# Threshold attention and a gated feed-forward layer on one core: the start of the feed-forward work moved from slot 20 to slot 22

## The chip, the cores and the metric

The kernel runs on one NeuronCore of a Trainium2 chip. Five engines work beside each other, each through its own list of instructions: TensorE (PE; its weight loads are shown as PEld), VectorE (DVE), ScalarE (ACT), GpSimd (POOL), and SyncE (SP), which here only issues DMA transfers. They meet through semaphores. Matmul results land in PSUM, eight banks of 2 KB per partition; PE alone writes matmul results there, and DVE and ACT read them out. The metric is device time in microseconds (us) of one execution.

## The reference

For each of 8 batches and 8 heads, with 576 tokens and head size 64, in f32:

```
scores = q k^T / sqrt(64)
thresh = max(scores, last axis) - tau
scores = where(scores >= thresh, scores, -1e9)
attn   = softmax(scores)
x      = attn v                 -> tokens x 512   (4608 tokens in all)
h      = x @ w_in               (512 -> 2048)
out    = (h * clip(h + 3, 0, 6) / 6) @ w_out      (2048 -> 512)
```

## The kernel before

**Slots.** Heads are taken two at a time (a pair) and pairs two at a time (a quad); a batch has two quads, and there are 16 quads. Each quad is cut into 9 slots: slots 0 to 3 are the first four 128-row blocks of queries of its first pair, 4 to 7 those of its second pair, and slot 8 holds the last 64 rows of both pairs. So there are 144 slots, numbered `n` = 0 to 143, and one loop over them writes the instructions of every engine in an order fixed by hand (`manual_schedule`). Within an engine that order is kept exactly; there is no scheduler behind it.

**One slot of attention.** `scores` (L288) makes the 128x576 scores of both heads of a pair in PSUM. `sm_max` (L303, DVE) copies them to the SBUF tile `s` and takes the row maximum; there are two such scans per slot. `sm_bias` (L308, POOL) makes the threshold, `sm_mask` (L312, ACT) rejects what is below it, `sm_exp` (L317, ACT) takes the exponential and its sum, `sm_recip` (L320, DVE) inverts the sum, and `sm_norm` (L325, POOL) writes the normalised rows as bf16 into `pn`. The pools of `s` and `pn` have four buffers each. The rows must then be transposed to `pT` (or `pR` for a slot 8): either by a DMA transpose on SP's queue (L333), or, where `on_chip` holds (L479), by nine PE transposes into PSUM (`pe_transpose`, L340) two slots later and one DVE copy (L341) in the slot after that. `av` (L349, L352) multiplies `pT` with `v`; DVE evicts the result into `xT` (L360) or `xR` (L370).

**The feed-forward work.** `mm1` (L384; L379 for the odd 64-row tails) multiplies a block of `xT` with `w_in` into one PSUM bank. One such item is eight matmuls of 128x256. `mm1_relu` reads the bank on ACT in even slots (L392) and on DVE in odd slots (L394), and `mm1_gate` (L407, DVE) writes `g`. `mm2_part` (L418) is a quarter of a 128-token output tile: four matmuls of 128x512; `second` issues one or more such parts in an even slot. The items wait in the list `todo1`, the parts in `todo2`: eight items of a batch enter `todo1` when the last pair of the batch has been multiplied with `v`, the rest after its tails (`multiply`). What is left after slot 143 is done in a tail.

**The two stages.** `N1` divides the loop. Up to slot `N1` the scores of slot n+2 are made in slot n and there is no feed-forward work. From slot `N1` each slot takes one item from `todo1`, the products with `v` are issued inside the slot instead of at its end, and an odd slot makes the scores of the two slots ahead; from `N1`+3 the scores of odd slots go to other columns of PSUM (`first`, `score_col`), which touch the lower halves of banks 2 and 5. `N2` is the last even slot in which ACT takes the exponentials before the relu of that slot. Banks 2 and 5 serve in turn (`bank`) for products with `v` and for the transposes of q and k. An item's bank is `HB` (6), `OB` (7), or bank 2 or 5, as L582 and L583 say; the parts of `mm2` collect in `OB`.

**Data movement.** `loads` holds the loads of q and k, issued one group per slot on SP behind that slot's transpose; for the fifth quad a group is four transfers of small rows. `casts` and `vcasts` hold the casting loads of the weights and of v, issued on POOL's queue behind that slot's `sm_norm`.

**Around slot 20.** In this version the items run in slots 20 to 35, there is none left for slots 36 and 37, and from slot 38 on there is one in every slot. Parts of `mm2` run in even slots from slot 28: two each in 28, 30, 32 and 34, three in 36, one in 38, two in 40, one in 42 and one in 44, sixteen in all; from slot 46 two each. `quad 1`'s second pair is multiplied with `v` in two halves of 256 columns (slots 18 and 21) and its tails in slot 23.

Of the kernel before, what the change touches and what calls it, by code (L numbers as in the profile page):

```python
# [20 lines left out]
def kernel(  # L21
# [18 lines left out]
    NSLOT = 9  # L40
    NB = 2
    N0 = 3
    N1 = 20
    N2 = 26
    HB, OB = 6, 7
    scale = 1.0 / math.sqrt(D)
    tau = float(tau)
# [30 lines left out]
    casts = []  # L78
# [93 lines left out]
    def start(jobs, n):  # L172
        for _ in range(min(n, len(jobs))):
            jobs.pop(0)()
# [35 lines left out]
    now = -1  # L210
    turn = 0
# [5 lines left out]


    def copy_out(out, in_):
        if 0 <= now < N1 + 4:  # L220
            nc.vector.tensor_copy(out=out, in_=in_)
        else:
            nc.scalar.copy(out=out, in_=in_)
# [48 lines left out]
    def first(n):  # L272
        return n > N1 + 2 and n % 2 == 1

# [32 lines left out]
    def sm_bias(sl):  # L307
        nc.gpsimd.tensor_scalar(out=sl.bias[:], in0=sl.m[:], scalar1=-scale, scalar2=tau, op0=Alu.mult, op1=Alu.add)  # L308
# [6 lines left out]
    def sm_exp(sl, i):  # L315
        s = sl.s[:, i, :]
        nc.scalar.activation(out=s, in_=s, func=Act.Exp, accum_out=sl.rsum[:, i:i + 1])  # L317
# [57 lines left out]
    def mm1(item, hb=HB):  # L375
        b, ni, c0 = item
        if c0 is None:
            for ki in range(KI):
                nc.tensor.matmul(ps[:, hb, :], xR[b // 2][:, ki, :], w_in_sb[:, ki, ni * P:ni * P + 512],  # L379
                                 start=(ki == 0), stop=(ki == KI - 1))  # L380
        else:
            for n in range(2):
                for ki in range(KI):
                    nc.tensor.matmul(ps[:, hb, n * 256:(n + 1) * 256], w_in_sb[:, ki, (ni + n) * P:(ni + n + 1) * P],  # L384
                                     xT[b][:, ki, c0:c0 + 256], start=(ki == 0), stop=(ki == KI - 1))
        return ps[:, hb, :]
# [27 lines left out]
    def mm2_part(bb, mt, part, ob=OB):  # L414
        if part == 0:
            o_ps[0] = ps[:, ob, :]
        for ni in range(part * 4, part * 4 + 4):
            nc.tensor.matmul(o_ps[0], gbuf[:, ni, mt * P:(mt + 1) * P], w_out_sb[:, ni, :],  # L418
                             start=(ni == 0), stop=(ni == NI - 1))
# [14 lines left out]
    todo2 = []  # L434
# [39 lines left out]
    queue = []  # L474
    for quad in range(NQUAD):
        for slot in range(NSLOT):
            sl = Slot()
            sl.quad, sl.slot, sl.n = quad, slot, len(queue)
            sl.on_chip = len(queue) < N1 - 3 and (slot in (1, 3, 5, 7, 8) or slot == 0 and quad > 0)  # L479
            queue.append(sl)  # L480
    scores(0)
    sm_max(queue[0])
# [17 lines left out]
    for quad in range(NQUAD):  # L500
        p0, p1 = 2 * quad, 2 * quad + 1
        if quad < NB:
            jobs = (((8, p0, 0, 512), (9, p1, 0, 256), (12, p1, 256, 256), (14, None, 0, 0)) if quad else
                    ((8, p0, 0, 512), (13, p1, 0, 512), (15, None, 0, 0)))
        else:
            jobs = [(7 - quad % 2 + 2 * i, *of) for i, of in enumerate(
                ((p0, 0, 256), (p0, 256, 256), (p1, 0, 256), (p1, 256, 256), (None, 0, 0)))]
        for after, *of in jobs:
            products.setdefault(quad * NSLOT + after, []).append((quad, *of))
# [10 lines left out]

    def second():
        nonlocal pieces, bb, mt, part
        pieces = min(len(todo2), {36: 3, 38: 1, 42: 1, 44: 1}.get(now, 2)) if now % 2 == 0 else 0
        for _ in range(pieces):
            bb, mt, part = todo2.pop(0)
            mm2_part(bb, mt, part)
# [3 lines left out]
    pieces = bb = mt = part = 0  # L530
    waiting = []
    for n, sl in enumerate(queue):
        quad, slot = sl.quad, sl.slot
        b, g = divmod(quad, 2)
        now = n
        if slot in (0, 4):
            pts[2 * quad + slot // 4] = pt_pool.tile([P, 9, 512], BF16, tag="pT", name="pT")
        if slot == 8:
            ptr[quad] = ptr_pool.tile([P, 9, P], BF16, tag="pR", name="pR")
        for ahead in {0: (1, 2), 9: (3,), 16: (4,)}.get(n, (quad + 2,) if quad > 2 and slot == (2 if quad == 3 else 0) else ()):  # L540
            if ahead < NQUAD:
                load_quad(ahead)
        if slot == 0 and g == 1 and b + 1 < B:
            load_v(b + 1)
        for copy in last_keys:
            copy()
        last_keys = []
        if 0 < n <= N1:
            for i in range(2):
                sm_exp(prev, i)  # L550
        if n + 1 < len(queue):
            if n <= N1 or n > N2 + 1 or n % 2 == 0:
                sm_max(queue[n + 1])
            sm_bias(queue[n + 1])
        even = n >= N1 and n % 2 == 0
        if n >= N0:
            sm_recip(prev)
        for copy in waiting:
            copy()
        waiting = []  # L560
        if N0 <= n <= N1:
            scores(n + 2)
            if n in (3, 6):
                warm_up(6)
        if even and n <= N2:
            sm_max(queue[n + 2])
        if n == N1:
            for i in range(2):
                sm_mask(sl, i)
        exp_first = even and n <= N2  # L570
        if exp_first:
            for i in range(2):
                sm_exp(sl, i)
        if n == N1:
            for i in range(2):
                sm_mask(queue[n + 1], i)

        if todo1 and n >= N1:
            item, then = todo1.pop(0)
            if n == len(queue) - 2:  # L580
                second()
            h = mm1(item, 0 if n == len(queue) - 1 else HB if n <= N1 or n % 2 == 0 or pieces > 1 else  # L582
                    (2, 5)[turn % 2] if pieces else OB)  # L583
            todo2.extend(then)
        else:
            item = None
        if n >= N1:
            for copy in multiply(n):
                copy()
        if item:  # L590
            mm1_gate(item, h, mm1_relu(h, on_act=even))
        if n > 1 and queue[n - 2].on_chip:
            waiting.append(pe_transpose(queue[n - 2]))
        if prev is not None and n < N0:
            sm_recip(prev)
            for copy in waiting:
                copy()
            waiting = []
        if n != len(queue) - 2:
            second()  # L600
        if n < N1:
            for i in range(2):
                sm_mask(sl, i)
        if n >= N1:
            if not exp_first:
                for i in range(2):
                    sm_exp(sl, i)
            if n != N1 and n + 1 < len(queue):
                for i in range(2):
                    sm_mask(queue[n + 1], i)  # L610
        if n < N1:
            waiting.extend(multiply(n))
        if part == 3:
            waiting.append(lambda tile=(bb, mt): late.extend(mm2_out(*tile, on_act=False)))
            part = 0
        evict = []
        for job, of in turns.get(n, ()):
            if job == "k":
                (last_keys if even else evict).append(transpose_k(of))
            elif job == "q":  # L620
                if of // 2 not in qkT:
                    alloc_qk(of // 2)
                (waiting if even else evict).append(transpose_q(of))
            else:
                (last_keys if even else evict).append(transpose_rest(of, of_k=of > 0))
        evict = [out_of_psum for out_of_psum in evict if out_of_psum]
        if N0 <= n < N1:
            waiting.extend(evict)
            evict = []
        for out_of_psum in evict:  # L630
            out_of_psum()
        if n == 0:
            warm_up(8)
        if n < N0:
            scores(n + 2)
            warm_up(6)
        elif n > N1 and n % 2:
            for m in (n + 3, n + 2):
                if m < len(queue):
                    scores(m)  # L640
        if n > 0:
            sm_norm(prev)
        flush()
        if n == 0:
            start(loads, 5)
        elif n not in (4, 12, 15, 18, 21) and not 23 < n < 30 and (n < 37 or n % 2 == 0):
            start(loads, 1)
        if n < 4 or 15 < n < 20 or n > 33:
            start(vcasts, 1 if n < N1 or n % 2 else 0)
        else:  # L650
            start(casts, 2 if n in (5, 8, 11, 14) or N1 <= n < N1 + 7 else 1)
        prev = sl

    last = NQUAD - 1
# [85 lines left out]
```

## Time and profile before

| what | value |
|---|---|
| time, median of 3 runs (lowest, highest) | 519.51 us (519.31, 520.68) |
| the profiled execution: its time, its span | 519.51 us, 517.7 us |
| PE busy, mean granted clock | 505.2 us (98%), 0.999 |
| ACT busy | 450.8 us (87%) |
| DVE busy | 441.5 us (85%) |
| POOL busy | 298.1 us (58%) |
| DMA transposes on SP's queue (`pT`, `pR`) | 119 + 15 |

Busy time is time in which an instruction of that engine was under way. Matmuls overlap in the array and their ends are modelled, so PE at 98% is not PE at its peak; how long a stretch of work takes is read from the starts of the groups. DVE and ACT instructions also overlap by about 0.1 us: two exponentials of one slot start 0.67 us apart.

### The profile page before, as it was taken

The page shows a single profiled execution, that of the slowest core. Times are in us where ns is not written, and L with a number is a line of the kernel's source. Part 1 is how long each engine was busy: PE and PEld are TensorE (multiplying, and loading weights), DVE is VectorE, ACT ScalarE, POOL GpSimd, SP SyncE. Part 2 cuts the span into 40 slices and gives each one's busy share as a digit, 9 for nine tenths or more (in the row PEclk, how much of TensorE's full clock was granted, in tenths as well). Part 3 has the DMA queues.
Part 4 walks back from the last instruction along what each step waited for, and adds up shares of the span by engine and source line. Part 5 has one row for each costly group of instructions (what it writes and reads, how often), then busy time and mean ns, then how long its engine had stood idle before and what let it go on. Part 6 is the DMA issues. An engine that isn't in the chain of part 4 may idle for free.

```text
span 517.7 us, 12082 instructions
## 1 busy us (share of the span) xinstructions
PE 505.2 (98%) x4126; PEld 320.6 (62%) x4126; DVE 441.5 (85%) x1125; ACT 450.8 (87%) x977; POOL 298.1 (58%) x536
## 2 busy tenths in 40 slices
PE   8999998999999999999999999999999999999996
PEld 6655565666655666666655666666655666667564
DVE  3788988998999999999999999999999999877261
ACT  3999987999999999999999999999999999986060
POOL 1788877756665666657566656657566655552000
PEclk9999999999999999999999999999999999999999
DMA  6999999989999999999899998999989996654122
GB/s 139 175 160 156 157 164 181 180 145 179 154 171 183 167 194 162 171 163 177 157 159 175 177 175 157 174 155 175 171 152 168 187 179 115 104 121 89 63 56 68
DMA packets 317870, 79.65 MB, mean 154 GB/s; under 512 B 300432, under 2 KB 312976, under 8 KB 317808
## 3 DMA queue, kind: packets, MB, share of 16 engines
q1 hardware_dynamic: 298304, 68.85, 79.3%
q0 software_dynamic: 18304, 9.64, 15.0%
q8 instruction: 32, 0.52, 0.4%
q10 hardware_dynamic: 1200, 0.39, 0.3%
q14 instruction: 30, 0.25, 0.1%
HBM read 36.70 MB, written 9.44 MB: 89 GB/s over the span
## 4 chain that ended last, share of the span: by engine, by line
PE 79%; DVE 5%; DMA 2%; ACT 2%; POOL 0%; issue 0%; POOLq 0%; DVEq 0%
PE ps L288 25%; PE ps L418 23%; PE ps L384 19%; PE ps L349 7%; PE ps L379 2%; DVE g L407 1%; PE ps L352 1%; DMA pT<-pn 1%; DVE s L303 1%; DMA g<-go 1%; DVE r L394 1%; PE ps L663 1%; ACT r L392 1%; ACT s L312 1%; ACT s L317 0%
## 5 line engine op out<-in xcount | busy, mean ns | idle before, releaser
L325 POOL TENSOR_SCALAR pn<-s,rinv 128x576 bf16<-128x576 f32 x288 | 210.7, 743 | 21.5 <-issue 4.5
L303 DVE TENSOR_SCALAR_CACHE_REDUCE s<-ps 128x576 f32<-128x576 f32 x288 | 205.1, 749 | 19.6 <-PE ps L288 8.4
L312 ACT ACTIVATE s<-s,bias 128x576 f32<-128x576 f32 x288 | 205.8, 762 | 7.0 <-POOL bias L308 6.5
L317 ACT ACTIVATE s<-s 128x576 f32<-128x576 f32 x288 | 192.5, 671 | 0.3
L288 PE MATMUL ps<-kT,qT 64*128 64x192 f32 (+7 forms) x1280 | 177.4, 419 | 3.4 <-DVE s L303 1.9
L288 PEld LDWEIGHTS ps<-kT,qT 64*128 64x128 f32 (+1 forms) x1280 | 104.7, 175 | 59.4 <-issue 15.6
L384 PE MATMUL ps<-xT,w_in_sb 128*128 128x256 bf16 x1024 | 131.1, 273 | 0.9 <-DVE g L407 0.8
L418 PE MATMUL ps<-w_out_sb,g 128*128 128x512 bf16 x560 | 131.0, 379 | 0.0
L384 PEld LDWEIGHTS <-w_in_sb 128*128 128x128 bf16 x1024 | 95.6, 98 | 40.7 <-issue 21.3
L308 POOL TENSOR_SCALAR bias<-m 128x2 f32<-128x2 f32 x144 | 26.9, 187 | 152.0 <-DVE rinv L320 136.7
L407 DVE SCALAR_TENSOR_TENSOR g<-r,ps 128x512 bf16<-128x512 f32 x128 | 87.7, 687 | 14.4 <-ACT r L392 10.5
L418 PEld LDWEIGHTS <-g 128*128 128x128 bf16 x560 | 54.5, 98 | 55.3 <-issue 0.7
L392 ACT ACTIVATE r<-ps,three 128x512 f32<-128x512 f32 x81 | 55.3, 686 | 27.3 <-PE ps L384 21.3
L317 ACT ACTIVATION_READ_ACCUMULATOR s<-s 128x1 f32 x288 | 54.5, 189 | 0.0
L394 DVE TENSOR_SCALAR r<-ps 128x512 f32<-128x512 f32 x63 | 42.9, 681 | 0.0
L349 PE MATMUL ps<-pT,vm 128*64 128x256 bf16 (+1 forms) x488 | 39.3, 283 | 0.8 <-DMA pT<-pn 0.8
L349 PEld LDWEIGHTS <-vm 128*64 128x64 bf16 x744 | 27.6, 110 | 17.3 <-issue 15.1
L360 DVE CAST xT<-ps 128x256 bf16<-128x256 f32 (+1 forms) x61 | 26.4, 432 | 9.3 <-PE ps L352 9.2
L426 DVE TENSOR_SCALAR osb<-ps 128x512 f32<-128x512 f32 x31 | 20.9, 673 | 8.4 <-PE ps L418 8.4
L303 DVE DVE_READ_ACCUMULATOR s<-ps 128x1 f32 x288 | 23.9, 83 | 0.0
L320 DVE RECIPROCAL rinv<-rsum 128x2 f32<-128x2 f32 x144 | 23.0, 160 | 0.7 <-ACT s L317 0.6
L144 POOL DMA_DIRECT2D vm<-in_v_dram x28 | 21.4, 766 | 0.1
(58 smaller groups left out, 253.4 us busy)
## 6 DMA issues: line engine op xcount, KB each, us to landing
out_dram<-osb SPq DMA_DIRECT2D x31, 256.0 KB, 2.6
nq<-in_q_dram SPq DMA_DIRECT2D x96, 72.0 KB, 3.4
km<-in_k_dram SPq DMA_DIRECT2D x96, 64.0 KB, 2.9
vm<-in_v_dram POOLq DMA_DIRECT2D x24, 128.0 KB, 4.0
km<-in_k_dram SPq DMA_DIRECT2D x16, 128.0 KB, 4.1
w_in_sb<-in_moe_w_in_dram POOLq DMA_DIRECT2D x16, 128.0 KB, 3.7
w_out_sb<-in_moe_w_out_dram POOLq DMA_DIRECT2D x16, 128.0 KB, 3.7
pT<-pn SPq DMA_TRANSPOSE x119, 3.9
```

The source lines that it names most:

```text
L288: nc.tensor.matmul(ps_flat[rows, c0:c0 + w], qT_of(pair)[a * 64:(a + 1) * 64, q0:q0 + rows.stop - rows.start], kT_of(pair)[a * 64:(a + 1) ...
L303: nc.vector.tensor_scalar(out=sl.s[:, i, :], in0=ps_flat[:, c0:c0 + S], scalar1=1.0, scalar2=None, op0=Alu.mult, op1=Alu.max, accum_out=sl ...
L308: nc.gpsimd.tensor_scalar(out=sl.bias[:], in0=sl.m[:], scalar1=-scale, scalar2=tau, op0=Alu.mult, op1=Alu.add)
L312: nc.scalar.activation(out=s, in_=s, func=Act.Prelu, bias=sl.bias[:, i:i + 1], scale=scale, alpha=REJECT)
L317: nc.scalar.activation(out=s, in_=s, func=Act.Exp, accum_out=sl.rsum[:, i:i + 1])
L325: nc.gpsimd.tensor_scalar(out=pn[:, i, :], in0=sl.s[:, i, :], scalar1=sl.rinv[:, i:i + 1], scalar2=1.0, op0=Alu.mult, op1=Alu.mult)
L349: nc.tensor.matmul(pb[a * 64:(a + 1) * 64, :], vm[:, 2 * hp + a, c * D:(c + 1) * D], pT[:, 5 * a + c, cols], start=(c == 0), stop=False)
L384: nc.tensor.matmul(ps[:, hb, n * 256:(n + 1) * 256], w_in_sb[:, ki, (ni + n) * P:(ni + n + 1) * P], xT[b][:, ki, c0:c0 + 256], start=(ki = ...
L392: nc.scalar.activation(out=r, in_=hps, func=Act.Relu, bias=three[:])
L394: nc.vector.tensor_scalar(out=r, in0=hps, scalar1=3.0, scalar2=0.0, op0=Alu.add, op1=Alu.max)
L407: nc.vector.scalar_tensor_tensor(out=out, in0=r, scalar=6.0, in1=hps, op0=Alu.min, op1=Alu.mult)
L418: nc.tensor.matmul(o_ps[0], gbuf[:, ni, mt * P:(mt + 1) * P], w_out_sb[:, ni, :], start=(ni == 0), stop=(ni == NI - 1))
```

## The change

`N1` goes from 20 to 22 and `N2` from 26 to 28, and the expressions that hang on them are adjusted:

```diff
-    N1 = 20
-    N2 = 26
+    N1 = 22
+    N2 = 28
...
-        if 0 <= now < N1 + 4:
+        if 0 <= now < N1 + 2:
...
-            sl.on_chip = len(queue) < N1 - 3 and (slot in (1, 3, 5, 7, 8) or slot == 0 and quad > 0)
+            sl.on_chip = len(queue) < N1 - 1 and (slot in (1, 3, 5, 7, 8) or slot == 0 and quad > 0)
...
-            jobs = (((8, p0, 0, 512), (9, p1, 0, 256), (12, p1, 256, 256), (14, None, 0, 0)) if quad else
-                    ((8, p0, 0, 512), (13, p1, 0, 512), (15, None, 0, 0)))
+            jobs = ((8, p0, 0, 512), (13 - 2 * quad, p1, 0, 512), (15 - 3 * quad, None, 0, 0))
...
-        pieces = min(len(todo2), {36: 3, 38: 1, 42: 1, 44: 1}.get(now, 2)) if now % 2 == 0 else 0
+        pieces = 2 if now % 2 == 0 and todo2 else 0
...
-            h = mm1(item, 0 if n == len(queue) - 1 else HB if n <= N1 or n % 2 == 0 or pieces > 1 else
-                    (2, 5)[turn % 2] if pieces else OB)
+            h = mm1(item, 0 if n == len(queue) - 1 else OB if n > N1 and n % 2 and not pieces else HB)
...
-            start(casts, 2 if n in (5, 8, 11, 14) or N1 <= n < N1 + 7 else 1)
+            start(casts, 2 if n in (5, 8, 11, 14) or 21 < n < 28 else 1)
```

What follows from it in the order of the instructions:

- Slots 20 and 21 belong to the first stage and have no item. The items run from slot 22 to slot 143 without a gap, so slots 36 and 37 have one each.
- Slots 17, 18 and 19 are transposed on the chip: three DMA transposes fewer on SP (one `pR`, two `pT`), three groups of nine PE transposes (in slots 19, 20 and 21) and three DVE copies (in slots 20, 21 and 22) more.
- `quad 1`'s second pair is multiplied with `v` in one piece in slot 20, its tails in slot 21.
- `mm2` begins in slot 30 with two parts, and has two parts in every even slot after that; by slot 46 both versions have issued sixteen.
- In odd slots after an even slot with one part (39, 43, 45) the item goes to bank 6 instead of bank 2 or 5. One call of `bank` fewer exchanges banks 2 and 5 for what follows.
- Slots 20 and 21 issue one weight load each instead of two; the last of `w_out` is issued in slot 29 instead of 28.
- Key copies are still made by DVE up to slot 23: `N1` + 4 before and `N1` + 2 after are both 24.
- From slot 46 to the end every engine has the same instructions in the same order as before.

## The prediction

> **What bounds the kernel now.** I read the page's busy times first:
>
> ```profile
> PE 505.2 (98%) x4126; PEld 320.6 (62%) x4126; DVE 441.5 (85%) x1125; ACT 450.8 (87%) x977; POOL 298.1 (58%) x536
> ```
>
> PE seems to be all, but it is so only from slot 46 on: in the waits of 160 to 440 us no matmul waits for anybody, and two slots take 6.39 us (184.48 to 190.87 below). The instructions from slot 46 on are unchanged, so the change is worth what it does to the start of slot 46, which is the item at 151.97. I split the way there at slot 30.
>
> Up to slot 30 the bound is ACT. Its timeline, from the exponentials that slot 20 begins with to the relu of slot 30:
>
> ```profile
> 63.00 0.67 ACT L317 ACTIVATE s<-s 128x576 f32<-128x576 f32 x1
> ...
> 69.20 0.69 ACT L392 ACTIVATE r<-ps,three 128x512 f32<-128x512 f32 x1 [0.43 <-PE ps L384]
> ...
> 74.86 0.69 ACT L392 ACTIVATE r<-ps,three 128x512 f32<-128x512 f32 x1 [0.99 <-PE ps L384]
> ...
> 87.18 0.67 ACT L392 ACTIVATE r<-ps,three 128x512 f32<-128x512 f32 x1
> 90.38 1.44 ACT L312 ACTIVATE s<-s,bias 128x576 f32<-128x576 f32 x2 [2.53 <-POOL bias L308]
> ...
> 101.16 0.69 ACT L392 ACTIVATE r<-ps,three 128x512 f32<-128x512 f32 x1 [0.30 <-PE ps L384]
> ```
>
> These 38.16 us hold 11 pairs of masks and 11 pairs of exponentials of 1.33 us each (start to start), five relus of 0.57 and a key copy of 0.47: 32.6 us of work, so 5.5 us of waiting. Nearly half is the one wait at 87.75. The timelines of POOL and of SP's queue show where it comes from:
>
> ```profile
> 87.56 1.46 POOL L325 TENSOR_SCALAR pn<-s,rinv 128x576 bf16<-128x576 f32 x2 [3.10 <-DMA pT<-pn]
> ```
> ```profile
> 66.07 2.60 SPq L333 DMA_TRANSPOSE pR<-pn  x1
> 68.84 1.28 SPq L333 DMA_TRANSPOSE pT<-pn  x1
> 70.58 2.35 SPq L95 DMA_DIRECT2D nq<-in_q_dram  x4
> 73.03 3.37 SPq L333 DMA_TRANSPOSE pT<-pn  x1
> 76.45 1.36 SPq L127 DMA_DIRECT2D kr<-in_k_dram  x2
> 77.85 2.66 SPq L100 DMA_DIRECT2D km<-in_k_dram  x4
> 80.61 12.65 SPq L333 DMA_TRANSPOSE pT<-pn  x6
> ```
>
> SP issues without a pause and is late: the rows of slot 20 are normalised by 72.3, and their transpose is issued at 80.61. POOL needs that `pn` buffer back for slot 24 and stands still; behind it waits its own threshold for slot 28 (through DVE, whose scan needs a free `s`), and for that ACT.
>
> From slot 30 on PE should be the bound. Its timeline, at the first group of slots 36 (two slots without an item), 38, 40, 42, 44 and 46, and later at slots 54, 56, 58 and 64:
>
> ```profile
> 119.85 2.76 PE L418 MATMUL ps<-w_out_sb,g 128*128 128x512 bf16 x12
> ...
> 125.44 1.05 PE L384 MATMUL ps<-xT,w_in_sb 128*128 128x256 bf16 x8
> ...
> 131.66 0.70 PE L288 MATMUL ps<-kT,qT 64*128 64x256 f32 x2 [0.54 <-DVE g L407]
> 132.29 1.05 PE L384 MATMUL ps<-xT,w_in_sb 128*128 128x256 bf16 x8
> ...
> 142.10 3.10 PE L288 MATMUL ps<-kT,qT 64*128 64x384 f32 x16
> 145.13 1.05 PE L384 MATMUL ps<-xT,w_in_sb 128*128 128x256 bf16 x8
> ...
> 151.97 1.04 PE L379 MATMUL ps<-w_in_sb,xR 128*128 128x512 bf16 x4
> ```
> ```profile
> 178.10 1.05 PE L384 MATMUL ps<-xT,w_in_sb 128*128 128x256 bf16 x8
> ...
> 184.48 1.05 PE L384 MATMUL ps<-xT,w_in_sb 128*128 128x256 bf16 x8
> ...
> 190.87 1.05 PE L384 MATMUL ps<-xT,w_in_sb 128*128 128x256 bf16 x8
> ...
> 210.17 1.05 PE L384 MATMUL ps<-xT,w_in_sb 128*128 128x256 bf16 x8
> ```
>
> Slots 38-39 and 44-45 have one part of `mm2` instead of two, 0.86 us less work, and yet take 6.85 and 6.84 us. Their odd item lies in bank 2 or 5, and the scores that follow (2.21 us elsewhere, 3.10 at 142.10) wait for its gate on DVE. That slack is what matters below.
>
> **The change, part by part.** Sums are made on the profiled execution: 519.51 us, 1.8 of it outside the span; it is also the median.
>
> *Two items fewer before slot 30.* ACT loses one relu (slot 20): -0.57. DVE loses two gates and one relu (3 x 0.61 to 0.71 = 2.0), PE two items (2 x 0.88); none of these two bound there.
>
> *Three transposes from SP to PE and DVE.* SP's queue loses 2.60 + 1.28 + 3.37 = 7.25 us of issue ahead of the transpose of slot 20. The loads of the fifth quad move up past them: q from 70.58 to about 66, the keys to 68.4-72.4. Slot 20's transpose can then go out when its rows are ready, by about 72.5 instead of 80.61, and with a median of 5.5 us to landing there it is in by 78. POOL wants the buffer at about 83. ACT's wait of 2.63 (87.75 to 90.38) goes: -2.63, bounds -2.63 and 0. Next in line is slot 21's transpose, ready near 74.4, with as much margin. PE gains three groups of nine transposes in slots 19, 20, 21; a group takes 0.68 us (38.06, 40.91, 43.45, 45.99, where slots of ACT still take 2.67). DVE gains three copies of 0.65, as much as the 2.0 it loses. In slot 20 PE now holds scores 1.24, transposes 0.68 and the 512-column product 1.2 (48.53 to 49.73): 3.1 us against ACT's slot of 2.66, so the scores of slot 23 come some 0.5 late. DVE's slots 20 and 21 hold 2.7 us each. The group is covered by ACT as long as these delays do not add up; I put 0.5 on the path, bounds 0 and 2 (three groups, uncovered).
>
> A rule that speaks against this: the Trainium skill, "TensorE: Matmul & The Clock Gate", section "Part 4: PE-mode transpose", gives about 275 ns to a 128x128 transpose inside a kernel and says that transposes do not keep the fast clock. The rows show nine in 0.68 us and a granted clock of 1.00 throughout 40 to 50 us, so the page's figure reads as a latency that overlaps. Paid one after the other, a group would be an estimated 2.48 us, 1.8 more than the row's, and three would cost 5.4.
>
> *The switch of stages* moves from slot 20 to 22. Its waits in ACT (0.34, 0.53, 1.09, 0.30, 0.19: 2.45 us) move with it. The biggest, 1.09 for the item of slot 22, follows scores that waited 0.66 for a key copy; after, no key block is transposed between (only tails in slot 22, copied at the start of 23). But DVE's slot 22 gets one copy, the odd tails (0.20) and a key copy (0.6) on top of four scans. I keep 2.45 less the 0.5 above; bounds -1.2 and +1.
>
> So the relu of slot 30 comes 0.57 + 2.63 = 3.2 earlier: at 98 instead of 101.16, and the item before it with it.
>
> *Exponentials before relu in slot 28* (`N2`): its relu is 1.33 later, but the next item goes to bank 7, so nobody waits. *Weights*: the last `w_out` tile is issued at POOL's slot 29 instead of 28, 3.7 us to landing, and is first used in slot 32 instead of 30: nothing, as one slot is 3.2. *The second pair's product* in one piece: the same columns, its copy 0.58 instead of 0.33 twice. *Banks 2 and 5 exchanged*: from 160 to 440 us only nine weight loads (1.8 us, under running matmuls) waited on them; 0, bounds -1 and +1.
>
> *Slots 30 to 46.* Slots 30 to 35 are as before (19.77; slots 48 to 53, of the same shape, 19.76). Slots 36 to 45 get two items (1.75 us) and two parts net (8 before, 10 after: 1.73) more, and so become what slots 54 to 63 are: 210.17 - 178.10 = 32.07 us. Before they take 151.97 - 119.85 = 32.12. So the 3.5 us cost 0: they fill the slack left by short bursts. Bounds -0.5 and +3.5. The output transfers on SP move too (the first from slot 31 to 33, 2.6 us to landing): nothing waits for them but three buffers, so 0.
>
> Sum: -0.57 - 2.63 + 0 = -3.2; 519.5 - 3.2 = **516.3 us**. All lower bounds together would give -5.9 and all upper ones +6.9; they will not all fall on one side, so the range below takes about two thirds of them.
>
> **Rivals.**
>
> *Slower: scans and scores become the chain.* In slots 19 to 22 the scan on DVE, the scores on PE and the next scan run in a loop of 2.54 us (65.45 to 67.99) just under ACT's 2.66. If all the added work lands in the loop, 3 x (0.68 + 0.65) = 4.0, and the heavier slot 22 adds 0.8, then 4.8 - 3.2 = +1.6, or 521.1; with a growing transition 522. For it: DVE was idle only 0.4 between scans there. Against: slots 9 to 12 hold a group and a copy each and keep to 2.54. It decides if the loop loses more than 3.2 us over slots 19 to 23.
>
> *Within 0.3%: the late slots have no slack.* If slots 38 to 45 are slow because DVE is full (its pair holds 6.3 us with an output copy), not for the bank, the added bursts cost up to 3.4: 519.7. Against: slots 54 to 63 carry as much at 6.39.
>
> *Within 0.3%: the transpose queue stays late.* If SP was held by traffic, not its own list, POOL's wait returns elsewhere: only the 0.57 is left, 518.9.
>
> **How the numbers follow.** A difference under 0.3% (1.6 us) can't be told from none. Chances: forecast (gain of 1.6 to 5) 0.68; slower rival 0.17; the two flat ones 0.09 and 0.06. The likeliest case's own range is 514.8 to 517.9. Below 514.8 I leave 0.05 and above 521.0 about 0.15. Faster 0.68, same 0.15, slower 0.17.
>
> **What would show it.** Right: no wait of POOL for a `pT` between 70 and 100 us; slot 30's item near 97 instead of 100.08; slots 36 to 46 in 32 us; afterwards 6.39 per pair, all shifted alike. Wrong: scans more than 3.3 us apart in slots 20 to 23; PE waiting for DVE's gates in slots 36 to 45; SP's transposes still issued 8 us after their rows.

## The result, and the profile after

The changed kernel takes 514.48 us (median of 3 runs, 514.0 to 514.75) where the kernel before takes 519.51 (519.31 to 520.68): a ratio of 0.9896 with a 95% interval of 0.987 to 0.9921, so it is faster by 5.0 us. The forecast was 516.3; the measured time lies 0.3 us below the lower end of the range, 514.8. The profiled execution of the new kernel is the median run itself: 514.48 us with a span of 512.7, against a span of 517.7 before.

The page's busy times hardly differ from before (PE -0.9 us, DVE +1.5, ACT and POOL -0.1), so the five microseconds are waits, and they have to be looked for stage by stage:

```profile
PE 504.3 (98%) x4143; PEld 320.9 (63%) x4143; DVE 443.0 (86%) x1127; ACT 450.7 (88%) x977; POOL 298.0 (58%) x536
```

Both traces were cut at the start of the first exponential (ACT, L317) of each slot:

```
stretch                            before   after    difference   forecast
start to slot 0                    11.42    11.94    +0.52         0
slot 0 to 20                       54.59    54.60    +0.01         0
slot 20 to 26                      19.83    18.64    -1.19        -0.57
slot 26 to 27                       6.34     3.70    -2.64        -2.63
slot 27 to 30                       9.56     9.14    -0.43         0
slot 30 to 46                      51.88    51.85    -0.03         0
slot 46 to 143                                       -0.09         0
behind slot 143 (the tail)         50.05    48.87    -1.18         0
span                              517.74   512.70    -5.03        -3.2
```

The first 0.52 belongs to the execution and not to the change: other executions start up to 0.14 us earlier and 1.03 later than the one of before, and a second profile of the changed kernel (e9 below) started 0.24 later still.

ACT's timeline after, from slot 21 on, beside the one the prediction showed:

```profile
75.55 0.69 ACT L392 ACTIVATE r<-ps,three 128x512 f32<-128x512 f32 x1 [0.55 <-PE ps L384]
...
86.52 0.67 ACT L392 ACTIVATE r<-ps,three 128x512 f32<-128x512 f32 x1
87.09 1.43 ACT L312 ACTIVATE s<-s,bias 128x576 f32<-128x576 f32 x2
...
97.45 0.69 ACT L392 ACTIVATE r<-ps,three 128x512 f32<-128x512 f32 x1
```

The mask behind the relu of slot 26 starts 0.57 us after it, with nothing in brackets, where it waited 2.53 us for POOL before. The wait of 0.99 for an item has become 0.55, and the relu of slot 30 does not wait for its item any more (0.30 before). SP's queue and POOL show the cover:

```profile
66.46 3.72 SPq L95 DMA_DIRECT2D nq<-in_q_dram  x4
70.22 1.76 SPq L127 DMA_DIRECT2D kr<-in_k_dram  x2
72.05 2.66 SPq L100 DMA_DIRECT2D km<-in_k_dram  x4
74.88 14.63 SPq L333 DMA_TRANSPOSE pT<-pn  x6
```
```profile
81.02 1.46 POOL L325 TENSOR_SCALAR pn<-s,rinv 128x576 bf16<-128x576 f32 x2
83.90 1.46 POOL L325 TENSOR_SCALAR pn<-s,rinv 128x576 bf16<-128x576 f32 x2
86.77 1.47 POOL L325 TENSOR_SCALAR pn<-s,rinv 128x576 bf16<-128x576 f32 x2
```

The transpose of slot 20 is issued at 74.88 instead of 80.61 (the forecast said 72.5: the loads in front of it take 8.1 us of SP, not 6.4), and POOL normalises slot after slot 2.87 us apart without waiting for a buffer.

PE's timeline after, first the groups that replace the three DMA transposes, then the first items of slots 30, 36, 38, 40 and 46:

```profile
66.10 0.68 PE L340 MATMUL ps<-identb,pn 128*128 128x128 bf16 x9
68.64 0.68 PE L340 MATMUL ps<-identb,pn 128*128 128x128 bf16 x9
71.62 0.68 PE L340 MATMUL ps<-identb,pn 128*128 128x128 bf16 x9
...
95.70 1.05 PE L384 MATMUL ps<-xT,w_in_sb 128*128 128x256 bf16 x8
...
116.14 1.05 PE L384 MATMUL ps<-xT,w_in_sb 128*128 128x256 bf16 x8
...
122.53 1.05 PE L384 MATMUL ps<-xT,w_in_sb 128*128 128x256 bf16 x8
...
128.91 1.05 PE L384 MATMUL ps<-xT,w_in_sb 128*128 128x256 bf16 x8
...
148.21 1.04 PE L379 MATMUL ps<-w_in_sb,xR 128*128 128x512 bf16 x4
```

The groups cost 0.68 us each, with the granted clock at 1.00 from 60 to 80 us. From slot 36 to slot 46 it is 148.21 - 116.14 = 32.07 us, and a pair of slots takes 6.39 from the start.

What nobody forecast is at the end. The tail of before (SP's transposes of `go`, the gates that write `go`, matmuls of the last items, and the last matmuls of all), and then the tail after:

```profile
495.67 7.46 SPq L409 DMA_TRANSPOSE g<-go  x2
500.58 1.29 DVE L407 SCALAR_TENSOR_TENSOR go<-r,ps 128x512 bf16<-128x512 f32 x2 [1.45 <-DMA g<-go]
501.32 1.91 PE L384 MATMUL ps<-xT,w_in_sb 128*128 128x256 bf16 x16 [0.16 <-DVE go L407]
...
510.18 3.66 PE L663 MATMUL ps<-w_out_sb,g 128*128 128x256 bf16 x32
```
```profile
491.82 6.47 SPq L409 DMA_TRANSPOSE g<-go  x2
495.41 3.66 PE L384 MATMUL ps<-xT,w_in_sb 128*128 128x256 bf16 x32
495.47 0.69 DVE L407 SCALAR_TENSOR_TENSOR go<-r,ps 128x512 bf16<-128x512 f32 x1 [0.17 <-ACT r L392]
...
505.81 3.66 PE L661 MATMUL ps<-w_out_sb,g 128*128 128x256 bf16 x32
```

`go` has one buffer. Its second writer waits until the first transpose of `go` has landed: 1.45 us before, and nothing after, although every engine's instructions there are the same. This shortens PE's way by 0.53 us: the last matmul ends 46.16 us after the first exponential of slot 143 before, and 45.63 after. The other 0.65 of the 1.18 lies behind that matmul, where the span goes on for 3.89 us before and for 3.24 after. The last output lands 2.18 and 2.19 us behind the matmul, so the difference is in the semaphores that the engines pass at the very end.

### The profile page after: what moved, and what is told of

Its sections match the earlier page's. It is cut to its first block, busy times and chain, and to the rows that moved or that the text cites. A ratio compares the mean times of both kernels' runs of the same rounds, so it can differ in the third digit from the quotient of the medians.

```text
span 512.7 us, 12126 instructions
## 1 busy us (share of the span) xinstructions
PE 504.3 (98%) x4143; PEld 320.9 (63%) x4143; DVE 443.0 (86%) x1127; ACT 450.7 (88%) x977; POOL 298.0 (58%) x536
## 4 chain that ended last, share of the span: by engine, by line
PE 80%; DVE 4%; ACT 3%; issue 1%; DVEq 0%
PE ps L288 24%; PE ps L418 23%; PE ps L384 20%; PE ps L349 7%; PE ps L379 3%; DVE s L303 1%; PE ps L352 1%; ACT s L317 1%; ACT s L312 1%; DVE g L407 1%; DVE r L394 1%; PE ps L661 1%; ACT r L392 1%; PE ps L340 0%; DVE xT L360 0%
## 5 line engine op out<-in xcount | busy, mean ns | idle before, releaser
L317 ACT ACTIVATE s<-s 128x576 f32<-128x576 f32 x288 | 192.5, 671 | 0.3
L288 PE MATMUL ps<-kT,qT 64*128 64x384 f32 (+7 forms) x1280 | 175.0, 419 | 2.7 <-DVE s L303 2.5
L288 PEld LDWEIGHTS ps<-kT,qT 64*128 64x128 f32 (+1 forms) x1280 | 103.2, 175 | 58.3 <-issue 16.0
L317 ACT ACTIVATION_READ_ACCUMULATOR s<-s 128x1 f32 x288 | 54.5, 189 | 0.0
```

The source lines that it names most:

```text
L288: nc.tensor.matmul(ps_flat[rows, c0:c0 + w], qT_of(pair)[a * 64:(a + 1) * 64, q0:q0 + rows.stop - rows.start], kT_of(pair)[a * 64:(a + 1) ...
```

## The experiments

Two theories stood at the start. Theory A is the prediction's own: the stall near 87 us goes because three transposes leave SP's list. The rival, B, is that the moved switch (two items fewer before slot 30, first burst in slot 30) does it. Beside them stood two smaller questions: whether short bursts were slow for their bank, and where the tail's 1.18 us come from. "Relative" means after the execution's own start offset is taken off; two executions of the unchanged kernel before differ by 0.46 us at slot 27, so a smaller difference between two traces says nothing; and e5 and e11, whose edits leave SP's list alone, will be seen to differ from before by 2.6 there.

**e1: the on-chip transposes alone**, in the kernel before.

```diff
-            sl.on_chip = len(queue) < N1 - 3 and (slot in (1, 3, 5, 7, 8) or slot == 0 and quad > 0)
+            sl.on_chip = len(queue) < N1 + 1 and (slot in (1, 3, 5, 7, 8) or slot == 0 and quad > 0)
```

> Before, with slots 17, 18, 19 (and only these in addition) transposed on the chip; the switch stays at slot 20. Theory A (SP's own list is late, its three transposes are what makes it late): POOL's wait for a pT near 87 us and ACT's 2.6 us behind it are gone, 516.9 us; up to 0.7 more where the groups of nine transposes stand beside items of the same bank in slots 20 and 21. Theory B (the gain before slot 30 comes from moving the switch, whatever SP does): 519.5 us.

Measured: 525.55 us (522.58 to 527.46) against 518.92, ratio 1.0113 (1.0064 to 1.0163). The granted clock differs between its runs: at 1.000 one took 522.58, 3.7 us more than the kernel before, and at 0.990 to 0.996 the other three took 524.39 to 527.46. In the profiled one it is 0.83 in 70 to 80 us and again in 80 to 90. Its waits between 60 and 152 us (total, times, longest):

```profile
ACT r L392 <- PE ps L384: 12.8, 8, 9.3
...
PE ps L384 <- DVE pT L341: 3.2, 2, 2.3
...
PE ps L340 <- DVE g L407: 2.4, 2, 1.5
```

The stall of POOL is gone, but in the second stage items and transposes use the same bank (6): a group waits for the gate of the item before it, the next item for the copy of the group, and that copy stands behind a key copy and two scans on DVE that wait for PE themselves (a group is done at 77.0, its copy starts at 81.15). ACT's relu of slot 22 then waits 9.3 us. So the transposes of slots 17 to 19 can be taken off SP only together with the switch. The edit could not price A's term by itself.

**e2: loads after the transposes.** The kernel before, with the fifth quad's loads moved down SP's list instead of the transposes taken off it.

```diff
-        elif n not in (4, 12, 15, 18, 21) and not 23 < n < 30 and (n < 37 or n % 2 == 0):
+        elif n not in (4, 12, 15, 18, 19, 20, 21) and not 23 < n < 30 and (n < 37 or n % 2 == 0):
```

> Before, with the fifth quad's loads of slots 19 and 20 (eight plus two transfers on SP) issued in slots 22 and 23 instead; all transposes stay DMA transposes, PE, ACT and DVE are untouched. Theory A (SP's list): some 6.4 us of issue leave the way of the transposes of slots 18 to 20, the wait of POOL near 87 us is gone, 516.9 us. Rival (the transposes are late because the DMA engines are full there, not because of SP's list): the wait stays over 1.5 us and the time within 0.8 us of 519.5.

Measured: 518.1 us (517.29 to 519.33), ratio 0.9985 (0.9968 to 1.0001). SP's queue:

```profile
69.03 9.69 SPq L333 DMA_TRANSPOSE pT<-pn  x4
78.78 2.44 SPq L95 DMA_DIRECT2D nq<-in_q_dram  x4
```

The transpose of slot 20 goes out at 72.52, POOL waits for no `pT`, and slot 27 comes a relative 2.64 earlier, just what the change brings there. By slot 46 1.97 of it are left, and in the medians 0.8, with an interval that touches 1. So in the kernel before, to have the transposes out early is enough to take the stall away. That SP's late list alone makes the stall does not follow (e5 and e11 below have the late list and no stall), and it is not sure that the gain lasts to the end.

**e3: the switch without the three transposes.** The kernel after, with `on_chip` cut where it was before.

```diff
-            sl.on_chip = len(queue) < N1 - 1 and (slot in (1, 3, 5, 7, 8) or slot == 0 and quad > 0)
+            sl.on_chip = len(queue) < N1 - 5 and (slot in (1, 3, 5, 7, 8) or slot == 0 and quad > 0)
```

> After, but slots 17, 18, 19 transposed by DMA as before; the switch stays at slot 22. Theory A: SP is late again, POOL waits for a pT again, 2.6 us of 5.0 are given back, 517.1 us; about 516.6 if the three groups of PE transposes cost 0.5. Theory B: 514.5 us or slightly less.

Measured: 515.27 us (514.56 to 516.84), ratio 0.9923 (0.9895 to 0.995). Relative to before: -1.35 at slot 26, -3.16 at slot 27, -3.62 at slot 46, where the change itself has -1.18, -3.82 and -4.28. Its waits between 60 and 152 us:

```profile
POOL pn L325 <- DMA pT<-pn: 1.3, 1, 1.3
...
ACT s L312 <- POOL bias L308: 1.1, 3, 0.7
PE ps L349 <- DMA pT<-pn: 0.9, 2, 0.5
PE ps L349 <- DMA pR<-pn: 0.9, 1, 0.9
```

Theory A fell as an account of the whole: without the on-chip part 85% of the gain at slot 46 is there, and the three groups add 0.66. The stall is not gone but small, 1.3 us for POOL where it was 3.1. Slot 20's transpose is still issued at 78.84, nearly as late as the 80.61 of before. POOL gets the buffer at 84.25 instead of 87.56: 1.8 of these 3.3 us are the earlier issue, 1.5 that POOL gets it 5.4 instead of 7.0 us after the issue. Neither is shown to come from the switch: the unchanged kernel issues it at 79.30 in its second execution (e4), and what the landing goes with stands under e11.

**e4 and e9: before and after once more, unchanged**, to see what repeats.

> Before, unchanged, for a second trace. After is 1.2 us shorter than before behind slot 143, where both have the same instructions: there before waits 1.45 us in DVE (4.8 us from issue to landing of a transposed go tile). If that landing is chance, this trace shows another wait, between 0 and 1.5 us, and the same -2.4 to -2.7 us of wait near 87 us; if it comes from the program, 1.4 us again. The first exponentials come at 11.4 us here and at 11.9 us after; the same question holds for them. Time 519.5 us, 518.3 where the tail has no wait.

> After, unchanged, for a second trace. If its parts are of the program and not of chance: against before, 1.2 us gained by the exponentials of slot 26, 3.5 to 3.9 by those of slot 27, 4.3 by slot 46, nothing between slots 46 and 143, and about 1 us behind slot 143 with no wait for the go transpose; 514.5 us.

Measured: e4 519.65 us (518.86 to 525.42), ratio 1.002 (0.9993 to 1.0047) to the other runs of the same kernel; e9 513.98 us (513.84 to 514.72), ratio 0.9893 (0.9836 to 0.9949). e9 has the same split as the first profile of the changed kernel: -1.18 at slot 26, -3.82 at slot 27, -4.30 at slot 46 and -1.18 in the tail. e4 has the stall, smaller by half a microsecond, and the wait in the tail. The first of these rows is from 60 to 152 us, the second from the tail:

```profile
POOL pn L325 <- DMA pT<-pn: 2.6, 1, 2.6
...
DVE go L407 <- DMA g<-go: 1.5, 1, 1.5
```

So the stall's size is partly chance: seven executions have SP's list of before, and POOL waits 2.0 to 3.1 us near 87 us in five of them (before, e4, e6, e7 and e8) and not at all there in two (e5 and e11). The rest of the split belongs to the program.

**e5: two buffers for `go`**, in the kernel before, paid for with two fewer of the small statistics tiles.

```diff
-    stat_pool = ctx.enter_context(tc.tile_pool(name="stat", bufs=6))
+    stat_pool = ctx.enter_context(tc.tile_pool(name="stat", bufs=4))
...
-    go_pool = ctx.enter_context(tc.tile_pool(name="go", bufs=1))
+    go_pool = ctx.enter_context(tc.tile_pool(name="go", bufs=2))
```

> Before, with two buffers of the go tile instead of one (and four instead of six of the small statistics tiles, to make room). Theory: the 1.5 us that DVE waits behind the last slot for the transpose of the first go tile to land is on the path; with a second buffer it goes, 1.2 us less than before at the end, nothing changes up to slot 143. Rival (the wait is covered by PE's own work there): no change.

Measured: 518.48 us (517.56 to 524.38), ratio 0.9996 (0.9971 to 1.002). The tail is 49.15 instead of 50.05, without the wait. But the trace shows something else too: the stall near 87 us is absent as well (-2.64 from slot 26 to 27), and still only 0.21 is left at slot 46. SP issues the transpose of slot 20 as late as before, yet POOL does not wait for its buffer. SP's queue, POOL's write of that buffer, and PE's timeline in slot 30:

```profile
79.51 14.63 SPq L333 DMA_TRANSPOSE pT<-pn  x6
```
```profile
84.71 1.47 POOL L325 TENSOR_SCALAR pn<-s,rinv 128x576 bf16<-128x576 f32 x2
```
```profile
102.45 0.38 PE L418 MATMUL ps<-w_out_sb,g 128*128 128x512 bf16 x1 [1.84 <-DMA w_out_sb<-in_moe_w_out_dram]
```

With the stall gone, the burst of slot 30 comes before the last tile of `w_out`. In the kernel before these weights were late enough to be the next wait; in the changed kernel that tile is first used a pair of slots later, and no PE wait for `w_out` shows. So a stall can go and bring nothing. With two causes changed in one trace, the median can't say what the buffer alone is worth.

**e6: the bank of short bursts**, in the kernel before: the odd item after a one-part burst goes to bank 6.

```diff
-            h = mm1(item, 0 if n == len(queue) - 1 else HB if n <= N1 or n % 2 == 0 or pieces > 1 else
-                    (2, 5)[turn % 2] if pieces else OB)
+            h = mm1(item, 0 if n == len(queue) - 1 else HB if n <= N1 or n % 2 == 0 or pieces else
+                    OB)
```

> Before, but in slots 39, 43 and 45 (behind an even slot with one part) the item goes to bank 6 instead of 2 or 5. Bank theory: the scores no longer wait for that item's gate; slots 38-39 and 44-45 fall from 6.85 us to 6.1 or less, 1 to 1.5 us less in all. Rival (DVE's work sets the pace of these slots): the pairs stay within 0.2 us of 6.85, and the time stays.

Measured: 517.43 us (516.95 to 518.05), ratio 0.9971 (0.9956 to 0.9987). PE's timeline from the item of slot 38 to that of slot 40:

```profile
124.88 1.05 PE L384 MATMUL ps<-xT,w_in_sb 128*128 128x256 bf16 x8
127.43 1.03 PE L384 MATMUL ps<-xT,w_in_sb 128*128 128x256 bf16 x8 [0.64 <-DVE g L407]
129.06 2.21 PE L288 MATMUL ps<-kT,qT 64*128 64x384 f32 x16
131.20 1.05 PE L384 MATMUL ps<-xT,w_in_sb 128*128 128x256 bf16 x8
```

The pair takes 6.32 us instead of 6.85, and its scores 2.21 in one group instead of 2.29 and 0.70 around a wait. The two short pairs give 0.95 together; 0.73 of the difference between the traces is a smaller stall and chance. So the wait of the scores was the bank's, as the prediction said. But 6.1 us or less was expected: the pair with one part still takes nearly the 6.39 of a pair with two, because the item of slot 39, now in bank 6, waits 0.64 for the gate that frees that bank. DVE is busy for 6.00 of the 6.32 us, so whether its pace would have set nearly the same time is not shown.

**e7: the fetch moved.** The kernel before, with 18 warm-up matmuls more on PE at the start (they compute nothing that is used).

```diff
-            if n in (3, 6):
-                warm_up(6)
+            if n in (3, 4, 5, 6):
+                warm_up(11 if n in (3, 6) else 4)
```

> Before, with 18 more warm-up matmuls (36 PE instructions with their weight loads) in slots 3 to 6, where PE waits for others. Theory: PE's instruction fetch of 16 KB, which falls on the DMA engines 2.8 to 3.7 us after the first go transpose is issued and delays that transpose's last packets (landing 4.8 us instead of 3.2), comes some 2.5 us earlier, before the transpose; DVE's wait of 1.5 us behind slot 143 is gone and the end is 1.2 us earlier; up to 0.5 us may be lost in slots 3 to 6. Rival (chance, or the order of the transposes): the wait stays at 1.5 us.

The page shows DMA transfers of instructions, 16 KB each, on a queue of their own, 32 in the run (`q8 instruction: 32, 0.52, 0.4%`). PE and PEld have 4126 instructions each, so 32 would be one for about every 258 of PE's, and that this queue is PE's is borne out below: 36 more instructions of PE move the fetch. Where such a fetch falls, by the packets of the queues, from the moment at which SP issues the first transpose of `go`:

```
kernel   fetch runs (us)   transpose lands   DVE waits   tail (us)
before   2.80 - 3.73       4.82              1.45        50.05
e4       2.85 - 3.80       4.85              1.5         50.05
e2       2.82 - 3.75       4.83              1.5         50.06
e6       2.84 - 3.79       4.84              1.5         50.06
e8       2.70 - 3.66       4.69              1.3         49.91
e12      2.61 - 3.49       4.67              1.3         49.88
after    0.36 - 1.28       3.09              none        48.87
e9       0.21 - 1.14       3.04              none        48.88
e10      0.16 - 1.14       3.02              none        49.22
e7       0.14 - 1.41       3.21              none        49.52
e3       3.78 - 4.79       3.05              none        49.15
e5       2.96 - 3.92       3.06              none        49.15
```

In the first six the last 2 of the transpose's 1056 packets run right behind the fetch, 0.9 us after the others. Where the fetch comes a microsecond earlier or later, or, as in e5, when the packets are through (2.60), the transpose lands at 3.0 to 3.2. e7 differs from before there in nothing but the position of the fetch, and its wait is gone: the wait is shown to be this. It is not the whole 1.18, though. In e7, as in e3, e5, e10 and after, the last matmul ends 45.63 us after the first exponential of slot 143, against 46.16 before, so the wait is worth 0.53, and that is all that e7's tail gains. From there to the end of the span it is 3.89 us in before and 3.90 in e7, 3.59 in e10, 3.52 in e3 and e5, 3.24 in after. Two things differ in this stretch, and they come singly too: SP passes one of its last nine semaphores before the last output lands in before, e3, e5 and e7, and six in e10 and after; and two semaphores of POOL lie 0.37 us apart in before, e7 and e10, 0.09 in e3, e5 and after. No run was made for this 0.65, and what sets it is open. As a version e7 is no gain: 520.24 us (518.82 to 522.32) against 519.23, ratio 1.0022 (1.0005 to 1.0039). The trace shows 0.53 won in the tail and 0.55 lost by slot 6, where the warm-ups stand.

**e8: the order of the bursts alone**, in the kernel before: no burst in slot 28, two parts in every even slot from 30, and the new bank rule.

```diff
-        pieces = min(len(todo2), {36: 3, 38: 1, 42: 1, 44: 1}.get(now, 2)) if now % 2 == 0 else 0
+        pieces = 2 if now % 2 == 0 and todo2 and now >= N1 + 10 else 0
...
-            h = mm1(item, 0 if n == len(queue) - 1 else HB if n <= N1 or n % 2 == 0 or pieces > 1 else
-                    (2, 5)[turn % 2] if pieces else OB)
+            h = mm1(item, 0 if n == len(queue) - 1 else OB if n > N1 and n % 2 and not pieces else HB)
```

> Before, with the parts of mm2 and the banks of the items as after has them (two in every even slot from 30 on, sixteen by slot 44), the switch and all else as before. Theory (before's early burst in slot 28 and the short bursts in 38 to 44 cost more than they bring): slots 28-29 lose 0.7 to 1.0 us, slots 36 to 45 another 1 to 1.7; 517.5 us against 519.3. Rival (only the switch and the transposes matter): within 0.5 us of before.

Measured: 517.6 us (516.75 to 519.9), ratio 0.9975 (0.996 to 0.999). Relative to before it is -0.96 at slot 27 (the stall, by chance), -1.24 at slot 30 and -2.43 at slot 46. The order is worth 1.47 of this: 0.28 in slots 28 and 29, where no gate is waited for now, 0.35 in slots 36 and 37, and 0.84 in slots 38 to 45, the short pairs of e6.

**e10: exponentials before the relu up to slot 26 only**, in the kernel after.

```diff
-    N2 = 28
+    N2 = 26
```

> After, with N2 at 26: in slot 28 the relu stands before the exponentials again, all else as after. Theory (nobody waits for that relu, the next item has another bank): within 0.3 us of after. Rival (the order in slot 28 is part of the gain): up to 1 us slower at slot 30.

Measured: 514.48 us (514.31 to 514.98), ratio 0.9908 (0.9874 to 0.9942), the time of the change itself; at slot 46 the traces differ by 0.15. The move of `N2` costs and brings nothing.

**e11: the weights' loads as after**, in the kernel before, to see whether fewer casts in slots 20 and 21 let the transposes land sooner, as e3's 5.4 us suggested.

```diff
-            start(casts, 2 if n in (5, 8, 11, 14) or N1 <= n < N1 + 7 else 1)
+            start(casts, 2 if n in (5, 8, 11, 14) or 21 < n < 28 else 1)
```

> Before, with one weight load instead of two in slots 20 and 21, as after issues them. Traffic theory (the transposes are late because the weight loads fill the DMA engines): POOL's wait for a pT near 87 us falls from 2.0 to 3.1 us to about 1.3, as in the run with the switch alone moved; PE may wait for the last weights in slot 30. Queue theory: the wait stays at 2.0 to 3.1 us. Time 519 us, 518 by the traffic theory if no weight is late.

Measured: 526.44 us (519.41 to 530.24), ratio 1.0074 (1.0019 to 1.0129). Its profiled execution ran at a lower granted clock (0.994; 0.82 in 100 to 110 us, 1.00 up to there), so beside its waits only what comes ahead of that is read. The wait near 87 us is gone: slot 27 comes 2.63 earlier than before. POOL's waits for `pT`, 4.0 us in three, end at 92.80, 99.25 and 103.94. PE waits for `w_out` 5.7 us in four, which shows again that in the kernel before the first bursts hang on the weights. This is what the traffic theory expected near 87 us, but it decides nothing, since e5 has no wait there either and its weights are loaded as before.

What the traces show instead is another fetch. For the transpose of slot 20, in the executions in which SP issues it late (times from the start of the span; landings from the DMA's semaphore):

```
kernel   issued   PE's fetch      lands   after the issue   POOL waits
before   80.61    85.05 - 86.17   87.38   6.8               3.1
e4       79.30    84.87 - 85.81   87.22   7.9               2.6
e6       79.61    84.51 - 85.46   86.78   7.2               2.3
e8       79.82    84.84 - 85.78   86.86   7.0               2.1
e7       82.79    80.10 - 81.59   87.46   4.7               2.0
e3       78.84    83.85 - 84.99   84.07   5.2               1.3
e5       79.51    84.17 - 85.12   84.36   4.8               none
e11      79.59    86.81 - 87.96   85.36   5.8               none
```

In the first four the fetch falls on the transpose, which lands 1.1 to 1.4 us after the fetch is through. In the others the fetch is over before the issue, or the transpose is in by 0.3 us after the fetch begins, and it takes 4.7 to 5.8 us. In the execution of before, SP's queue starts some 250 to 285 packets of data in each quarter of a microsecond from 84.5 to 85.5 us, and 3 to 9 from 85.75 to 87.0. So the stall goes with two things: how late SP issues, and whether a fetch falls on the transfer. The first is shown by e2; the second is read from eight traces, of which only e7's edit was made to move the fetch. In the changed kernel the transpose is issued at 74.88 and lands at 80.41, ahead of the fetch at 82.69.

**e12: e8's edit and e2's edit together**, to see whether the parts add up without the switch.

> Before, with the fifth quad's loads of slots 19 and 20 in slots 22 and 23 and with the parts of mm2 and the banks of after: two single edits together, the switch still at 20. If they add up: 2.0 and 1.5 us, 3.5 at slot 46, of the 4.3 that after gains there; with the wait for the go transpose behind slot 143, 516.0 us. What is missing to after is then the switch's own: 0.8 us. Rival (both edits take away the same wait): 2.0 to 2.3 at slot 46, 517.3 us.

Measured: 516.95 us (515.86 to 518.15), ratio 0.9952 (0.9931 to 0.9973). At slot 46 it is -2.78 where e2's 1.97 and e8's 1.47 would have made -3.4, because a later transpose is now late: in the waits between 60 and 152 us

```profile
PE ps L349 <- DMA pT<-pn: 2.2, 1, 2.2
POOL pn L325 <- DMA pT<-pn: 2.1, 1, 2.1
```

The loads that were moved down are in front of the next transposes. Against the change's -4.28 at slot 46 1.5 us are missing. What the change has and e12 does not is above all the switch two slots later, and with it the three on-chip transposes and the order of the weights' loads; which of these brings the 1.5 is not shown by e12. No version beat the changed kernel.

## Why the prediction was right, and where it was not

Right was the direction, and with it the reading by stages. ACT sets the pace up to slot 30; the big wait behind slot 26's relu went entirely (-2.64, forecast -2.63), though that the numbers agree so well is luck, since a second execution of the kernel before has 0.46 us less of this wait; slots 36 to 46 take 32.07 us, the very number worked out from slots 54 to 63; and the 3.5 us of added PE work are covered by the slack of short bursts, of which e6 and e8 show a part, some 0.5 us a pair, to have been the wait for bank 2 or 5. The three transposes stayed cheap: 0.68 us a group at a granted clock of 1.00. This disagrees again with the price in the Trainium skill, "TensorE: Matmul & The Clock Gate", section "Part 4: PE-mode transpose", about 275 ns for one transpose in a kernel, by which nine would take an estimated 2.48; the measurement decides. The one lower clock beside such groups is e1's (0.83 in 70 to 90 us), where PE also waits 0.85 to 2.35 us around them, so it does not tell which of the two it goes with. The slower rival, scans and scores as the chain, did not come: the first scans of slots 20 to 24 start at most 3.13 us apart (68.67 to 71.80), below the 3.3 named. Nor did the flat ones: the late slots had slack, and POOL's wait did not return elsewhere.

Three steps failed.

*"The instructions from slot 46 on are unchanged, so the change is worth what it does to the start of slot 46".* The tail was put at nothing by this and gave 1.18 of the 1.8 us by which the median missed. The instructions are unchanged, but their place in the instruction stream is not. By the tail PE has executed 34 instructions more, so the fetch that used to run at 2.80 to 3.73 us behind the transpose of `go` runs at 0.36 to 1.28, and the second writer of `go` waits for nothing: 0.53 us. The trace of before showed both the wait and the fetch; nobody who took the tail as common would have looked. The other 0.65 came behind the last matmul, in the order and the spacing of the closing semaphores, and its cause is open.

*"I keep 2.45 less the 0.5 above"* for the waits of the switch, and with it "0.5 on the path" for the three groups. ACT's waits between slots 20 and 26 fell from 1.70 to 1.08 us (0.43 + 0.99 + 0.18 + 0.10 in the timeline before, 0.26 + 0.55 + 0.17 + 0.10 after), where the sum left them as they were: slots 20 to 26 gave 1.19 instead of 0.57, one relu and 0.6 of waits. Slots 27 to 30 gave 0.43 more, which the sum did not have: without the burst in slot 28 the item behind it does not wait for a gate, nor the relu of slot 30 for its item (e8 has 0.28 there). The bound of -1.2 given for the switch covers both. The term was mis-sized by 1.0 us.

*The working for "Three transposes from SP to PE and DVE",* which put the whole -2.63 down to three DMA transposes leaving SP's list. The size is right and the cause is too narrow. e2 shows that an early issue, got by the order of SP's list alone, removes the stall. But a late issue does not always bring it: e5 and e11 issue as late as e4 and do not stall, and the traces put the difference to a fetch that falls on the transpose or misses it. In e3, with the switch moved and the transposes left on SP, POOL's wait is 1.3 us instead of 3.1 and ACT's 0.7 instead of 2.5, and the three groups are worth 0.66 at slot 46 in the end. And e1 shows that this part can't be had alone: in the second stage it costs more than it brings (3.7 us in the run at full clock).

The sum against the span: +0.53 (up to slot 20) - 1.19 - 2.64 - 0.43 - 0.03 - 0.09 - 1.18 = -5.03.

What stays open: the 0.65 us behind the last matmul; how much of e3's smaller stall belongs to the moved switch; and a run that moves the fetch near 85 us and nothing else, which would turn the table under e11 from a reading into a proof.

## What to carry to other kernels

Work that starts earlier gains nothing if its supply sets the end: both kernels have done the same items and parts by slot 46, and what the earlier start took was slots of the stage that ACT bounds, and short bursts in a bank that the scores need. A stall is worth its length only if what is behind it is ready (e5 lost 2.3 of the same 2.6 us again, in part to weights that came late), so one asks for the next late thing before one counts a wait as gained. And "the same instructions from here on" is not "the same time from here on": an edit that shifts an engine's instruction count shifts its fetches, and a wait of a microsecond far behind the edit can come or go with it.

## What the hardware showed

- An instruction fetch of PE (16 KB, 0.9 to 1.3 us in the table of e7) delays a DMA transpose that is under way: the last 2 of its 1056 packets wait until the fetch is through, and the transpose lands after 4.67 to 4.85 us instead of 3.0 to 3.2. In six of the executions in the table it did so and in six it did not, and the position of the fetch goes with it in each. Under load the same shows for the transpose of slot 20: 6.8 to 7.9 us from issue to landing in the four executions in which the fetch falls on it, 4.7 to 5.8 in the other four of e11's table.
- A DMA transpose takes SP from 1.25 to 3.37 us to issue (slots 17 to 27 of the kernel before), and two executions of that same program issue the one of slot 20 at 80.61 and at 79.30 us and have it in after 6.8 and 7.9 us. A margin of one or two microseconds behind such a transpose is none.
